# Loads of q and k issued two chunks ahead, and the first strided stores, the mask and half of the first values put on GpSimd's queue

## The chip, the cores and the metric

The kernel runs on one core of one Trainium2 chip. The metric is the device time in microseconds (us) of one execution, lower is better. The kernel before takes 826.1 us in the median of three runs (820.74 to 828.68). The core has five instruction streams that run side by side: PE (TensorE: matrix multiplies and transposes), ACT (ScalarE), DVE (VectorE), POOL (GpSimd) and SP (SyncE, which only issues transfers here). Each stream is in order: an instruction that waits holds everything behind it on its own engine.

## The reference

Attention with two kinds of windows feeds a mixture of experts with one expert per token, and that feeds a last layer with a rational activation. Cut to what matters:

```
scores = q k^T / 8, for 4 batches, 8 heads, 576 positions, 64 elements a head
heads 0-3: each position sees the last 32 positions
heads 4-7: each position sees every fourth of the last 128
attn = softmax(scores) ; x = attn v, rows of 512 elements, 2304 tokens
logits = x w_gate + modality_bias ; e = argmax(logits)
x = gate * relu(x w1[e]) w2[e]          # 8 experts, 512 -> 1024 -> 512
h = x w_in ; g = P(h) / (Q(h) + 1e-6) ; out = g w_out
```

## The kernel before

**Chunks.** The attention runs over 8 chunks. A chunk is two batches and two heads; its kind (table `CHUNKS`, line 34) is 1 for the strided heads and 0 for the plain ones. Chunks 0 and 1 are strided, 2 and 3 plain, 4 and 5 strided, 6 and 7 plain. Chunks 0 to 3 belong to batches 0 and 1 (`bp` 0), the others to batches 2 and 3 (`bp` 1). `load(c)` (line 408) brings q and k of a chunk into a pair of tiles from the pool `ald`, which has two buffers (line 388), so a chunk's tiles can be filled when the chunk two before it has been read for the last time. A strided chunk comes as rows of 2 KB (72 partitions), a plain one as pieces of 256 bytes. `load_values(c)` (line 427) brings v into one of two buffers `vws`; for strided heads one call brings all four heads (`load_v_dil`, 12 transfers), for plain heads two at a time (`load_v`, 2 transfers). `halo(c)` (line 449) then copies, on POOL, the last 32 rows of each block to the top of the next one.

**The loop.** 36 steps g (line 635) each work on 4 tiles of 64 positions. A step issues up to two parts of `qk_T` (PE transposes of the loaded q or k, ACT copies them out), `step_s` for tile group g (scores on PE, mask and maximum on DVE, line 489), `step_e` for g-1 (exponentials on ACT), `step_t` for g-2 (transposes on PE), `step_v` for g-3 (product with v on PE, line 515, and scaling on DVE into the tile `xu`, line 529). When four heads of a batch pair are done, `put_x` (line 585) stores `xu` to the DRAM tensor `x_rows`: for strided heads as 20 transfers on SP, because neighbouring positions of a head lie four rows apart in `x_rows`; `xu` has two buffers. `gate_tasks` puts the router's work between the steps. At the end of a step, the loop decides which loads to issue: `load(done_L)` once 8(done_L-1) parts of `qk_T` have been issued (line 679), values once the steps have come far enough (line 682).

**Order.** The block is scheduled by hand: each engine runs its instructions in the order in which the code issues them. Transfers issued by SP and ACT share eight completion semaphores (DMAHW0 to DMAHW7 in the rows of order below). A transfer that is given a semaphore first waits until the transfer that held it before has landed; usually that is the one eight before it. Transfers issued by POOL have eight of their own (DMASW).

**Start.** `load(0)` issues q on SP and k on ACT, in halves (one head, both batches), with the mask on ACT between them; then come the 12 transfers of the first values and `load(1)` on SP. `spin` runs empty multiplies on PE between the first parts of `qk_T` (`SPIN`, line 84).

**End of the attention.** After the last step ACT issues the two halves of the first expert's second weight, `raw20` and `raw21` (1 MB each, `fetch2`, line 213), and then runs the last `step_e` (line 696). The rest of the kernel, from about 160 us on, is the experts and the last layer; their first weights and gathers are released by the router's result.

Of the kernel before, what the change touches and what calls it, by code (L numbers as in the profile page):

```python
# [18 lines left out]
B, H, S, D = 4, 8, 576, 64  # L19
NTOK = B * S  # L20
DM = H * D
QT, WIN, KT = 64, 32, 96
NJ = S // QT
# [7 lines left out]
CQ = 16  # L31
RUNS = ((0, 2), (2, 3), (3, 4), (4, 5), (5, 6), (6, 7), (7, 9))
# [51 lines left out]
SPIN = (12, 0, 1, 0)  # L84
# [82 lines left out]
def fused(ctx, tc, io):  # L167
# [215 lines left out]
    with ExitStack() as actx, tc.manual_schedule(), nc.allow_low_precision(reason="integers"):  # L383
# [24 lines left out]
        def load(c):  # L408
            bp, _, kind, h0 = CHUNKS[c]
            raw[c] = [ld.tile([72, 2, 2, 8 * D] if kind else [QT, 2 * NJ, 2, D], F32, tag="ld" + nm, name="ld" + nm) for nm in "qk"]  # L410
            bs = slice(2 * bp, 2 * bp + 2)
            if c == 0:
                for hh in range(2):
                    for t, src, eng in zip(raw[c], (q, k), (nc.sync, nc.scalar)):
                        eng.dma_start(out=t[:, hh], in_=src[bs, h0 + hh].rearrange("b (p j) d -> p b (j d)", j=8))
                    if hh == 0:
                        nc.scalar.dma_start(out=mask[:, 0:NP0], in_=io["mask"][:, 0:NP0])
                return
            for t, src in zip(raw[c], (q, k)):
                for bb in range(2):  # L420
                    x = src[2 * bp + bb, h0:h0 + 2]
                    if kind:
                        nc.sync.dma_start(out=t[:, :, bb, :], in_=x.rearrange("h (p j) d -> p h (j d)", j=8))
                    else:
                        nc.sync.dma_start(out=t[:, :, bb, :], in_=x.rearrange("h (j a) d -> a (h j) d", a=QT))
# [8 lines left out]
        def load_v_dil(bp, vw):  # L434
            for j in range(NJ):
                for lo, hi in pieces(QT * j, QT * j + QT):
# [5 lines left out]
                    nc.sync.dma_start(out=vw[a:a + hi - lo, :, j, 1:1 + 2 * D], in_=src)  # L442
# [142 lines left out]
        def put_x(c):  # L585
            bp, _, kind, _ = CHUNKS[2 * c]
            xu = xus.pop(c)
            cols = slice(DM // 2 * kind, DM // 2 * kind + DM // 2)
            for hf in range(2):
                xb = xu[64 * hf:64 * hf + 64].rearrange("a j h d -> a j (h d)")  # L590
                if not kind:
                    b = 2 * bp + hf
                    nc.sync.dma_start(out=x_dram[b * S:(b + 1) * S, cols].rearrange("(j a) e -> a j e", a=QT), in_=xb)
                    continue
                rr = x_dram[2 * bp * S:(2 * bp + 2) * S, cols].rearrange("(b m r) e -> b r m e", b=2, r=4)
                for j0, j1 in RUNS:
                    for lo, hi in ([(QT * j0, QT * j1)] if j1 - j0 == 2 else pieces(QT * j0, QT * j1)):
                        sg, m = divmod(lo, SEG)
                        bb, r2 = divmod(sg, 2)
                        dst = rr[bb, 2 * r2 + hf, m:m + hi - lo]  # L600
                        if j1 - j0 == 2:
                            nc.sync.dma_start(out=dst.rearrange("(j a) e -> a j e", a=QT), in_=xb[:, j0:j1])
                        else:
                            a = 64 * hf + lo - QT * j0
                            nc.sync.dma_start(out=dst, in_=xu[a:a + hi - lo, j0].rearrange("a h d -> a (h d)"))
# [10 lines left out]
        halo(0)  # L616
        load(1)
        load_values(1)
        halo(1)
# [15 lines left out]
        for g in range(NG):  # L635
# [43 lines left out]
            if done_L < NC and done_T >= 8 * (done_L - 1):  # L679
                load(done_L)  # L680
                done_L += 1
# [950 lines left out]
```

## Time and profile before

| | |
|---|---|
| median of 3 runs | 826.1 us (820.74 to 828.68) |
| the profiled execution | 826.8 us, of which the span from the first to the last instruction is 825.0 us |
| mean granted TensorE clock | 0.979 of full |
| PE busy | 791.3 us (96%) |
| PE weight loads busy | 638.4 us (77%) |
| DVE, ACT, POOL busy | 577.6, 509.7, 149.0 us |
| transfers | 73509 packets, 91.58 MB |

"Busy" adds up the time in which an engine had an instruction at work; times in the rows count from the span's start. The chain of waits is followed back from the last instruction of the kernel, so what stands in it held up the end. The attention takes about the first 140 us of the span; the change touches nothing behind it.

### The profile page before, as it was taken

The page shows a single profiled execution, that of the slowest core. Times are in us where ns is not written, and L with a number is a line of the kernel's source. Part 1 is how long each engine was busy: PE and PEld are TensorE (multiplying, and loading weights), DVE is VectorE, ACT ScalarE, POOL GpSimd, SP SyncE. Part 2 cuts the span into 40 slices and gives each one's busy share as a digit, 9 for nine tenths or more (in the row PEclk, how much of TensorE's full clock was granted, in tenths as well). Part 3 has the DMA queues.
Part 4 walks back from the last instruction along what each step waited for, and adds up shares of the span by engine and source line. Part 5 has one row for each costly group of instructions (what it writes and reads, how often), then busy time and mean ns, then how long its engine had stood idle before and what let it go on. Part 6 is the DMA issues. An engine that isn't in the chain of part 4 may idle for free.

```text
span 825.0 us, 15207 instructions
## 1 busy us (share of the span) xinstructions
PE 791.3 (96%) x5277; PEld 638.4 (77%) x5279; DVE 577.6 (70%) x1370; ACT 509.7 (62%) x993; POOL 149.0 (18%) x191
## 2 busy tenths in 40 slices
PE   7899997899998999999989999999999999999995
PEld 4777765687786678888768888888888888999894
DVE  3776788932252224895599987887788888888894
ACT  4655666234253325663689878777687678778783
POOL 2011008421110101231174512000020002001001
PEclk9998899999999999999999999999999999999998
DMA  7968947195947686774011001200020001001001
GB/s 189 160 145 150 191 147 199 51 339 211 333 153 288 247 306 209 236 276 158 18 39 39 14 1 38 66 1 1 0 69 22 1 0 65 1 1 38 1 1 38
DMA packets 73509, 91.58 MB, mean 111 GB/s; under 512 B 33577, under 2 KB 43323, under 8 KB 73403
## 3 DMA queue, kind: packets, MB, share of 16 engines
q1 hardware_dynamic: 68531, 76.38, 32.7%
q0 software_dynamic: 3360, 11.03, 3.8%
q10 hardware_dynamic: 1512, 2.91, 1.1%
q8 instruction: 48, 0.79, 0.4%
q14 instruction: 58, 0.48, 0.2%
HBM read 75.59 MB, written 14.71 MB: 109 GB/s over the span
## 4 chain that ended last, share of the span: by engine, by line
PE 83%; DMA 8%; DVE 4%; ACT 3%; issue 1%; SPq 0%; POOL 0%; POOLq 0%; ACTq 0%; DVEq 0%
PE p1t L1363 8%; PE p1t L1364 8%; PE p1t L1365 8%; DMA sw<-in_w 5%; PE p1t L146 4%; PE p1t L150 4%; PE p1t L148 4%; PE pht L1533 4%; PE pht L1534 3%; PE pht L1535 3%; PE pot L777 3%; PE pot L775 3%; PE pot L779 3%; PE pot L1535 2%; PE pxt L1533 2%; PE pxt L1534 2%
## 5 line engine op out<-in xcount | busy, mean ns | idle before, releaser
L1481 ACT ACTIVATE raw<-p1t 128x512 f32<-128x512 f32 (+1 forms) x78 | 43.2, 554 | 81.9 <-PE p1t L1365 77.0
L1488 DVE TENSOR_TENSOR raw<-raw,raw 128x512 f32<-128x512 f32 (+1 forms) x80 | 52.0, 649 | 59.0 <-ACT raw L1482 58.2
L768 DVE TENSOR_TENSOR hl<-pht,hh 128x512 fp32r<-128x512 f32 x34 | 21.9, 685 | 97.9 <-ACT hh L767 92.7
L1365 PE MATMUL p1t<-yh,wl 128*128 128x512 f32 (+1 forms) x240 | 89.0, 371 | 0.0
L1544 POOL DMA_INDIRECT out<-hs,row x10 | 10.9, 1087 | 302.2 <-ACT hs L1542 300.8
L1482 ACT ACTIVATE raw<-raw,bab 128x512 f32<-128x512 f32 (+1 forms) x80 | 61.9, 773 | 2.7
L1363 PE MATMUL p1t<-yh,wh 128*128 128x512 f32 (+1 forms) x160 | 59.6, 372 | 0.3 <-DVE m L1499 0.3
L1364 PE MATMUL p1t<-yl,wh 128*128 128x512 f32 (+1 forms) x160 | 59.2, 370 | 0.0
L1510 DVE SCALAR_TENSOR_TENSOR m<-m,nab,raw 128x512 f32<-128x512 f32 (+1 forms) x80 | 58.6, 733 | 0.1
L146 PE MATMUL p1t<-w1h,xh 128*128 128x512 f32 x144 | 57.7, 401 | 0.1
L150 PE MATMUL p1t<-w1h,xl 128*128 128x512 f32 x144 | 56.7, 393 | 0.0
L148 PE MATMUL p1t<-w1l,xh 128*128 128x512 f32 x144 | 56.4, 392 | 0.0
L1508 DVE SCALAR_TENSOR_TENSOR raw<-raw,raw 128x512 f32<-128x512 f32 (+1 forms) x80 | 56.4, 705 | 0.0
L1483 ACT ACTIVATE raw<-p1t,nab 128x512 f32<-128x512 f32 (+1 forms) x78 | 56.1, 719 | 0.0
L1490 ACT ACTIVATE raw<-raw,bab 128x512 f32<-128x512 f32 (+1 forms) x80 | 53.7, 671 | 0.5 <-DVE raw L1488 0.4
L1499 DVE SCALAR_TENSOR_TENSOR m<-m,nab,p1t 128x512 f32<-128x512 f32 (+1 forms) x78 | 53.5, 685 | 0.1
L775 PE MATMUL pot<-w2h,hh 128*128 128x512 f32 x128 | 52.0, 406 | 0.0
L777 PE MATMUL pot<-w2l,hh 128*128 128x512 f32 x128 | 51.6, 403 | 0.0
L1506 DVE SCALAR_TENSOR_TENSOR raw<-raw,raw 128x512 f32<-128x512 f32 (+1 forms) x80 | 51.6, 645 | 0.0
L1497 DVE TENSOR_TENSOR m<-raw,p1t 128x512 f32<-128x512 f32 (+1 forms) x78 | 49.3, 632 | 2.7
L779 PE MATMUL pot<-w2h,hl 128*128 128x512 f32 x128 | 50.6, 395 | 0.0
L489 DVE CUSTOM_DVE_ANT_0 pe<-sc,mask 128x96 f32<-128x96 f32 x144 | 28.4, 253 | 31.6 <-PE sc L485 19.6
(374 smaller groups left out, 2110.5 us busy)
## 6 DMA issues: line engine op xcount, KB each, us to landing
sw<-in_w SPq DMA_DIRECT2D x80, 256.0 KB
raw<-in_w SPq DMA_DIRECT2D x10, 1024.0 KB
dr<-in_w_in SPq DMA_DIRECT2D x16, 512.0 KB
dr<-in_w_out SPq DMA_DIRECT2D x16, 512.0 KB
y<-ys_rows SPq DMA_DIRECT2D x18, 256.5 KB
ldq<-in_q SPq DMA_DIRECT2D x16, 288.0 KB
ys_rows<-yo SPq DMA_DIRECT2D x17, 256.5 KB
ldk<-in_k SPq DMA_DIRECT2D x14, 288.0 KB
```

The source lines that it names most:

```text
L146: nc.tensor.matmul(out=p, lhsT=xh[:, kk], rhs=wh[n][:, kk], start=(kk == 0), stop=False)
L148: nc.tensor.matmul(out=p, lhsT=xh[:, kk], rhs=wl[n][:, kk], start=False, stop=False)
L150: nc.tensor.matmul(out=p, lhsT=xl[:, kk], rhs=wh[n][:, kk], start=False, stop=(kk == 3))
L775: nc.tensor.matmul(out=p, lhsT=a[:, c], rhs=w2h[n][:, kk], start=(c == 0), stop=False)
L777: nc.tensor.matmul(out=p, lhsT=a[:, c], rhs=w2l[n][:, kk], start=False, stop=False)
L779: nc.tensor.matmul(out=p, lhsT=b[:, c], rhs=w2h[n][:, kk], start=False, stop=(c == 7))
L1363: nc.tensor.matmul(out=p[:, 0:n], lhsT=wh(kk)[:, cs], rhs=ab[0][:, kk, 0:n], start=(kk == 0), stop=False)
L1364: nc.tensor.matmul(out=p[:, 0:n], lhsT=wh(kk)[:, cs], rhs=ab[1][:, kk, 0:n], start=False, stop=False)
L1365: nc.tensor.matmul(out=p[:, 0:n], lhsT=wl(kk)[:, cs], rhs=ab[0][:, kk, 0:n], start=False, stop=(kk == 3))
L1482: nc.scalar.activation(out=v, in_=ah, func=AF.Identity, scale=bab[:, 1:2], bias=bab[:, 0:1])
L1508: nc.vector.scalar_tensor_tensor(out=v, in0=v, scalar=2.0, in1=r, op0=ALU.subtract, op1=ALU.mult)
L1510: nc.vector.scalar_tensor_tensor(out=m, in0=m, scalar=nab[:, 0:1], in1=v, op0=ALU.add, op1=ALU.mult)
```

## The change

The diff, with lines of the loop that are only indented anew left out. `load(0)` issues quarters (one head, one batch) and the mask goes first, on POOL. Of the first values, odd blocks j go through POOL's queue. The strided `put_x` stores both halves (the two heads' parity rows) of a block with one transfer where the block lies within one segment, so 18 transfers instead of 20, and for batches 0 and 1 on POOL's queue. `halo(0)` is issued behind `load(1)`. `load(done_L)` is issued one chunk earlier in the code. The number of buffers in the pool `ald` isn't in the diff: it is two in both kernels.

```diff
-SPIN = (12, 0, 1, 0)
+SPIN = (12, 2, 2, 2)
...
             if c == 0:
+                nc.gpsimd.dma_start(out=mask[:, 0:NP0], in_=io["mask"][:, 0:NP0])
                 for hh in range(2):
-                    for t, src, eng in zip(raw[c], (q, k), (nc.sync, nc.scalar)):
-                        eng.dma_start(out=t[:, hh], in_=src[bs, h0 + hh].rearrange("b (p j) d -> p b (j d)", j=8))
-                    if hh == 0:
-                        nc.scalar.dma_start(out=mask[:, 0:NP0], in_=io["mask"][:, 0:NP0])
+                    for bb in range(2):
+                        for t, src, eng in zip(raw[c], (q, k), (nc.sync, nc.scalar)):
+                            eng.dma_start(out=t[:, hh, bb], in_=src[2 * bp + bb, h0 + hh].rearrange("(p j) d -> p (j d)", j=8))
                 return
...
         def load_v_dil(bp, vw):
             for j in range(NJ):
+                eng = nc.gpsimd if bp == 0 and j % 2 else nc.sync
...
-                    nc.sync.dma_start(out=vw[a:a + hi - lo, :, j, 1:1 + 2 * D], in_=src)
+                    eng.dma_start(out=vw[a:a + hi - lo, :, j, 1:1 + 2 * D], in_=src)
...
-                for j0, j1 in RUNS:
-                    for lo, hi in ([(QT * j0, QT * j1)] if j1 - j0 == 2 else pieces(QT * j0, QT * j1)):
...
+            eng = nc.sync if bp else nc.gpsimd
+            rr = x_dram[2 * bp * S:(2 * bp + 2) * S, cols].rearrange("(b m r) e -> b r m e", b=2, r=4)
+            for j in range(NJ):
+                parts = pieces(QT * j, QT * j + QT)
+                for lo, hi in parts:
+                    sg, m = divmod(lo, SEG)
+                    bb, r2 = divmod(sg, 2)
+                    dst = rr[bb, 2 * r2:2 * r2 + 2, m:m + hi - lo]
+                    if len(parts) == 1:
+                        eng.dma_start(out=dst, in_=xu[:, j].rearrange("a h d -> a (h d)"))
+                        continue
+                    for hf in range(2):
+                        a = 64 * hf + lo - QT * j
+                        eng.dma_start(out=dst[hf], in_=xu[a:a + hi - lo, j].rearrange("a h d -> a (h d)"))
...
-        halo(0)
         load(1)
         load_values(1)
+        halo(0)
         halo(1)
...
-            if done_L < NC and done_T >= 8 * (done_L - 1):
+            if done_L < NC and done_T >= 8 * (done_L - 2):
                 load(done_L)
```

SP's queue before, from the load of chunk 2 on (`ldq`, `ldk` are the tiles of q and k, `vw1` and `vw0` the two buffers of values; 64x18x64 is a plain chunk, 72x2x512 a strided one):

```order
L425 DMA ldq_302<-in_q 64x18x64 x2
L425 DMA ldk_303<-in_k 64x18x64 x2
L446 DMA vw1_153<-in_v 64x18x64 x2
L425 DMA ldq_551<-in_q 64x18x64 x2
L425 DMA ldk_552<-in_k 64x18x64 x2
L446 DMA vw1_153<-in_v 64x18x64 x2
L423 DMA ldq_816<-in_q 72x2x512 x2
L423 DMA ldk_817<-in_k 72x2x512 x2
L602 DMA x_rows_57<-xu_392 64x2x256
L605 DMA x_rows_57<-xu_392 16x256
```

Behind these come the other stores of `xu` (20 in all), the 12 transfers of the next values, and only then chunk 5. The same place on SP's queue in the change:

```order
L422 DMA ldq_277<-in_q 64x18x64 x2
L422 DMA ldk_278<-in_k 64x18x64 x2
L422 DMA ldq_317<-in_q 64x18x64 x2
L422 DMA ldk_318<-in_k 64x18x64 x2
L444 DMA vw1_153<-in_v 64x18x64 x4
L420 DMA ldq_570<-in_q 72x2x512 x2
L420 DMA ldk_571<-in_k 72x2x512 x2
L420 DMA ldq_831<-in_q 72x2x512 x2
L420 DMA ldk_832<-in_k 72x2x512 x2
L440 DMA vw0_152<-in_v 64x4x128 x2
```

Chunks 2 and 3 now stand ahead of both loads of plain values, chunks 4 and 5 ahead of the next strided values, and the stores of `xu` are gone from this queue. They stand on POOL's queue in the change, between small copies and the halo copies of the next strided values (`vw0`):

```order
L260 CAST tok16_97<-cst_82 128x9
L602 DMA x_rows_57<-xu_407 2x64x256 x2
L606 DMA x_rows_57<-xu_407 16x256 x2
L606 DMA x_rows_57<-xu_407 48x256 x2
L602 DMA x_rows_57<-xu_407 2x64x256
L606 DMA x_rows_57<-xu_407 32x256 x4
L602 DMA x_rows_57<-xu_407 2x64x256
L606 DMA x_rows_57<-xu_407 48x256 x2
L606 DMA x_rows_57<-xu_407 16x256 x2
L602 DMA x_rows_57<-xu_407 2x64x256 x2
L451 COPY vw0_152<-vw0_152 32x8x128 x4
```

Before, the four halo copies of `vw0` followed the small copies directly. On ACT, at the end of the loop, the two halves of the first expert's second weight and the last exponentials, before:

```order
L213 DMA raw20_2278<-in_w2 128x4x512
L213 ISA
L213 DMA raw21_2279<-in_w2 128x4x512 [waits DMAHW5_49]
L496 ACTIVATE pe_2346<-pe_2346,mx_2347 128x96 [waits DVE_49] x4
L130 ACTIVATE w1h1_2272<-raw11_66 128x512 [waits DMAHW4_49,DMAHW3_49,DMAHW0_49]
```

And in the change:

```order
L211 DMA raw20_2283<-in_w2 128x4x512 [waits DMAHW5_49]
L211 ISA
L211 DMA raw21_2284<-in_w2 128x4x512 [waits DMAHW5_49]
L494 ACTIVATE pe_2351<-pe_2351,mx_2352 128x96 [waits DVE_49] x4
L128 ACTIVATE w1h1_2277<-raw11_66 128x512 [waits DMAHW7_49,DMAHW6_49,DMAHW3_49]
```

Before, the two halves held different semaphores (`raw20` DMAHW7, `raw21` DMAHW5). In the change both hold DMAHW5, so `raw21` waits until `raw20` has landed, and the exponentials stand behind it.

## Rows read from the trace of the kernel before

**Rows 1.** The page's chain that ended last, by engine.
```profile
PE 83%; DMA 8%; DVE 4%; ACT 3%; issue 1%; SPq 0%; POOL 0%; POOLq 0%; ACTq 0%; DVEq 0%
```

**Rows 2.** Stretches: bounds, length, busy us (count) by engine, PE clock, DMA share, GB/s.
```profile
59.60:69.10 9.50, 9.50 (x175) 8.30 (x176) 8.29 (x52) 7.80 (x27) 0.00 (x0) 1.00 0.42 115
76.20:89.90 13.70, 13.16 (x130) 9.70 (x126) 5.80 (x31) 5.52 (x18) 0.00 (x0) 0.50 1.13 172
126.00:136.00 10.00, 7.26 (x89) 5.36 (x89) 8.60 (x35) 7.14 (x18) 9.32 (x10) 0.83 0.82 269
```

**Rows 3.** The chain's pieces in the attention: start us, us, what.
```profile
1.86 8.95 DMA ldk<-in_k
14.92 5.59 DMA ldk<-in_k
22.63 6.59 DMA ldq<-in_q
69.72 5.65 DMA ldq<-in_q
131.41 1.02 PE pt L503 x4
```

**Rows 4.** SP's transfers in order of time: start us, us, line, count.
```profile
13.87 1.01 SPq L423 DMA_DIRECT2D ldq<-in_q  x2
21.91 1.45 SPq L425 DMA_DIRECT2D ldq<-in_q  x2
...
44.67 0.63 SPq L602 DMA_DIRECT2D x_rows<-xu  x1
...
59.63 6.77 SPq L442 DMA_DIRECT2D vw<-in_v  x9
...
69.14 0.96 SPq L423 DMA_DIRECT2D ldq<-in_q  x2
```

**Rows 5.** DVE's first mask operation of steps 16, 20, 24 and 25.
```profile
60.25 0.26 DVE L489 CUSTOM_DVE_ANT_0 pe<-sc,mask 128x96 f32<-128x96 f32 x1
70.94 0.26 DVE L489 CUSTOM_DVE_ANT_0 pe<-sc,mask 128x96 f32<-128x96 f32 x1 [0.39 <-PE sc L485]
90.31 0.26 DVE L489 CUSTOM_DVE_ANT_0 pe<-sc,mask 128x96 f32<-128x96 f32 x1 [2.10 <-ACT pe L496]
94.03 0.25 DVE L489 CUSTOM_DVE_ANT_0 pe<-sc,mask 128x96 f32<-128x96 f32 x1
```

**Rows 6.** PE: the product of step 12, the router's multiply, two waits for q.
```profile
47.67 0.69 PE L515 MATMUL pv<-vw,pts 96*64 96x65 f32 x16
69.42 0.85 PE L562 MATMUL lgp<-xT,wg 128*32 128x384 f32 x6
73.65 0.47 PE L463 MATMUL pq<-ident,ldq 72*128 72x72 f32 x4 [1.22 <-DMA ldq<-in_q]
```

**Rows 7.** POOL: halo copies, the last small copy, its only transfers before 130 us.
```profile
36.07 2.02 POOL L453 COPY vw<-vw 32x1024 f32<-32x1024 f32 x2 [16.99 <-DMA vw<-in_v]
47.92 2.02 POOL L453 COPY vw<-vw 32x1024 f32<-32x1024 f32 x2 [9.83 <-DMA vw<-in_v]
...
51.52 0.20 POOL L262 CAST tok<-cst 128x9 f16<-128x9 f32 x1
...
123.88 1.14 POOL L365 DMA_INDIRECT xg<-x_rows,idx  x1 [16.14 <-DVE mx L489]
125.32 0.96 POOL L365 DMA_INDIRECT xg<-x_rows,idx  x1 [0.31 <-PE pg L549]
```

**Rows 8.** ACT and SP at the end of the attention.
```profile
126.97 0.42 ACTq L213 DMA_DIRECT2D raw<-in_w  x1
129.37 1.17 ACT L496 ACTIVATE pe<-pe,mx 128x96 f32<-128x96 f32 x4 [0.46 <-DVE mx L489]
...
133.34 4.22 SPq L605 DMA_DIRECT2D x_rows<-xu  x7
```

**Rows 9.** SP's own waits, 100 to 140 us: us in total, times, longest.
```profile
SPq L605 <- DMA raw<-in_w: 20.4, 2, 16.5
```

More of the change, by code (lines that the diff above doesn't have):

```diff
@@ L28 @@
 HP = HT + 1
-CQ = 16
-RUNS = ((0, 2), (2, 3), (3, 4), (4, 5), (5, 6), (6, 7), (7, 9))
 KINDS = ((1, 1, 0, 0), (1, 1, 0, 0))
@@ L410, in load @@
             raw[c] = [ld.tile([72, 2, 2, 8 * D] if kind else [QT, 2 * NJ, 2, D], F32, tag="ld" + nm, name="ld" + nm) for nm in "qk"]
-            bs = slice(2 * bp, 2 * bp + 2)
             if c == 0:
+                nc.gpsimd.dma_start(out=mask[:, 0:NP0], in_=io["mask"][:, 0:NP0])
                 for hh in range(2):
-                    for t, src, eng in zip(raw[c], (q, k), (nc.sync, nc.scalar)):
-                        eng.dma_start(out=t[:, hh], in_=src[bs, h0 + hh].rearrange("b (p j) d -> p b (j d)", j=8))
-                    if hh == 0:
-                        nc.scalar.dma_start(out=mask[:, 0:NP0], in_=io["mask"][:, 0:NP0])
+                    for bb in range(2):
+                        for t, src, eng in zip(raw[c], (q, k), (nc.sync, nc.scalar)):
+                            eng.dma_start(out=t[:, hh, bb], in_=src[2 * bp + bb, h0 + hh].rearrange("(p j) d -> p (j d)", j=8))
                 return
@@ L588, in put_x @@
             cols = slice(DM // 2 * kind, DM // 2 * kind + DM // 2)
-            for hf in range(2):
-                xb = xu[64 * hf:64 * hf + 64].rearrange("a j h d -> a j (h d)")
-                if not kind:
+            if not kind:
+                for hf in range(2):
                     b = 2 * bp + hf
-                    nc.sync.dma_start(out=x_dram[b * S:(b + 1) * S, cols].rearrange("(j a) e -> a j e", a=QT), in_=xb)
-                    continue
-                rr = x_dram[2 * bp * S:(2 * bp + 2) * S, cols].rearrange("(b m r) e -> b r m e", b=2, r=4)
-                for j0, j1 in RUNS:
-                    for lo, hi in ([(QT * j0, QT * j1)] if j1 - j0 == 2 else pieces(QT * j0, QT * j1)):
[L598 to L605, printed above, removed]
+                    nc.sync.dma_start(out=x_dram[b * S:(b + 1) * S, cols].rearrange("(j a) e -> a j e", a=QT),
+                                      in_=xu[64 * hf:64 * hf + 64].rearrange("a j h d -> a j (h d)"))
+                return
+            eng = nc.sync if bp else nc.gpsimd
[9 more added lines that the diff above has]
+                        continue
+                    for hf in range(2):
+                        a = 64 * hf + lo - QT * j
+                        eng.dma_start(out=dst[hf], in_=xu[a:a + hi - lo, j].rearrange("a h d -> a (h d)"))
         for i in range(NB):
```

## The prediction

> **What bounds the kernel now.** I read the chain of waits first. Over the whole span it runs on PE for 83% and through transfers for 8% [rows 1]; the question is where in the attention those transfers hold PE up, because the change touches nothing behind it. The pieces of the chain show four such places [rows 3]. The second half of the first k is issued at 1.86 and lands at 10.81. The k of chunk 1 is issued at 14.92 and lands at 20.51. The q of chunk 2 (22.63) lands at 29.22. The q of chunk 5 (69.72) lands at 75.37. The first three are one string. SP can't issue chunk 1 before 13.87 [rows 4], because five loads of the first values still stand ahead of it when the first k lands: (13.87 - 10.82) / 5 = 0.61 us each. Chunk 2's q, at 21.91 [rows 4], waits for chunk 1's last k, whose completion semaphore it takes.
>
> The fourth place is the costly one. Chunk 5 is issued only at 69.14, behind the stores that began at 44.67 and the values that began at 59.63 [rows 4]. PE then waits 1.22 us for it [rows 6], and from 76.2 to 89.9 its granted clock is 0.50, that is 1.2 GHz, with PE busy for 13.16 of 13.70 us [rows 2]. Just before, from 59.6 to 69.1, PE had been busy all the time at full clock while the 16 transfer engines were used for 0.42 [rows 2]. So there the transfers are late because of the order on SP's queue and the waits in it, not because the engines are full.
>
> What that costs is read off DVE's first mask operation, one per step. From step 16 to step 20 a step takes (70.94 - 60.25) / 4 = 2.67 us. From step 20 to step 25 the five take 94.03 - 70.94 = 23.09 us [rows 5]. Undisturbed I expect four at 2.67, one router multiply of 0.85 [rows 6], and the last at the 94.03 - 90.31 = 3.72 us that it already takes at full clock: 15.25. The place costs 7.8 us. Its lower bound, half of the slowed PE time alone, is 13.16 / 2 = 6.6.
>
> **The change part by part.** All sums are against the profiled execution, 826.8 us with a span of 825.0; the median of the runs shown, 826.1, is 0.7 lower.
>
> *Start: quarters, mask on POOL, half of the values on POOL, more spins.* Quarters let PE begin before 6.9 us, but that gain isn't kept: PE still waits for chunk 2's q in step 7, and what counts is when SP issues chunk 1. Eight of the twelve loads of values remain on SP, and only the last of them still needs a semaphore that the late q and k hold. So four fewer stand behind the landing: 4 x 0.61 = 2.4 us. The last quarter of q may land a little ahead of the last half of k, up to 0.9 more. Against it, POOL's four loads now share the transfer engines with q and k; that is at worst their own share of the time, 1 us. Bounds 1.4 to 3.3; I take **2.6**. The five extra spins fill time in which PE would wait. The same 2.6 carries through the string to step 8, since its members wait for each other.
>
> *Loads two chunks ahead.* The code issues them earlier, but the pool still has two buffers. A load therefore waits on SP for the last transposes of the chunk two before, as now, and what moves is only the order. What this frees: chunk 5 now waits for chunk 3's last transposes, about 58 - 2.6 = 55 us, instead of 69.14. It has about 15 us to land, where the four transfers of chunk 1 took 8 us beside other work. The wait at 73.65 and the slow clock behind it should go: **7.8**.
> What it delays: the first plain values, now behind chunk 3. Chunk 2's q, k and values needed 36.07 - 21.91 = 14.2 us and chunk 3's 47.92 - 36.07 = 11.9 [rows 4, 7]. Two thirds of the latter, 7.9, now go first, so these values land at 36.07 - 2.6 + 7.9 = 41.4, and one halo copy of 1.0 us later step 12 can use them. It wants them at 47.67 - 2.6 = 45.1 [rows 6]. Cost nothing, with 2.7 us to spare. The stores of chunks 2 and 3 and the plain values of chunk 6 stand behind chunk 7's load, which can go when chunk 5 is read out, near 80. By the same rates the load takes 7.9 and the values 4.0, and I allow 3 for the stores: 95. Step 30 wants these values five steps of about 3 us behind step 25 (94.03 - 10.4 = 83.6), near 98.6. Again no cost.
>
> *Stores on POOL.* SP loses 20 stores that took it from 44.67 to 59.6. POOL gets 18, behind its halo copies and small copies. Those end at 51.72 now [rows 7], so at 49.1. The next halo copies, which step 21 needs, stand behind the stores, and so does the release of the buffer of `xu`. Step 21's mask would run at 70.94 + 2.67 - 2.6 = 71.0 and its product with the new values 0.6 later, at 71.6 (an estimate: four transposes lie between). With a time r per store, the copy must fit: 49.1 + 18 r + 1.0 <= 71.6, r <= 1.19. No row shows a direct store issued by POOL. The nearest are two indirect transfers of 128 rows: 0.96 and 1.14 us, 1.44 from start to start [rows 7]. Twelve of the 18 stores have 16 to 48 rows, so I take r = 1.0 and **no cost**, with 3 us of room. At 1.44 the copy is 4.5 us late; then PE idles again and part of the 7.8 goes with it.
>
> A page of the Trainium skill speaks against this part. "DMA: Bandwidth & Descriptors", section "Issuing engines are not separate DMA queues", holds that issuing from several engines saves only the sequencer's time, usually small beside the transfer. The transfer engines at 0.42 while chunk 5 stands in SP's queue say that here it isn't small [rows 2, 4]. By that rule alone, the place at 70 us would stay as it is.
>
> *End of the attention.* Here the order shows a new wait. `raw21` now takes the semaphore that `raw20` holds, so ACT stands still until `raw20` has landed, and the last exponentials wait behind it. Now `raw20` is issued at 126.97 and the exponentials run at 129.37 [rows 8]. With both halves in flight `raw20` lands at 133.3, where a store on SP that waited for it goes on [rows 8, 9]: 6.4 us, the upper bound. Alone, 1.05 MB at the 269 GB/s of this stretch [rows 2] take 3.9, the lower. I take 5.0: ACT is free at 132.0, with its second issue (0.42) at 132.4, 3.0 later than now. PE's transposes at 131.41 [rows 3] follow the end of the exponentials (130.54) with 0.9 to spare, so 2.1 us are lost, and some at the low clock that PE already has there (0.83 on average [rows 2]). I take **2.5**, bounds 1 to 5. `raw21` itself isn't needed sooner.
>
> *Later strided stores (batches 2, 3).* 18 transfers instead of 20 on SP, far ahead of their use. Nothing.
>
> **Sum.** 2.6 + 7.8 - 2.5 = 7.9 us gained: 826.8 - 7.9 = **818.9 us**. Behind the attention everything is released by the router's result, so I let the gain through whole.
>
> **The rivals.**
> - *POOL is a little slow (r from 1.2 to 1.5).* Its stores take the place of the removed wait in step 21: up to 4.8 us of idle PE, and the clock may fall as it did behind 1.2 us of waiting. For it: indirect transfers 1.44 apart. Against it: twelve short stores. 818.9 + 4 = 823, or with the slow clock (6.6 us) up to 829.
> - *POOL is slow (r near 2): slower than before.* One mechanism: 18 stores end at 85.1 and the halo copy at 86.1, 14.5 us behind step 21's need. 818.9 + 14.5 + 4 of slow clock = 837. It decides from r = 1.6, where the copy is late by the 7.9 us of the gain. Against it: no transfer on POOL in these rows takes 2 us.
> - *Transfers are hidden or bound anyway; the change does not do what it says.* The two buffers forbid a real lead of two chunks. If the engines, busy for 1.13 of their time (summed over transfers) from 76 to 90 us [rows 2], are the limit, chunk 5 stays late and only start and end change: 826.8 - 2.6 + 2.5 = 826.7. Against it the 0.42.
> - *The start gains more and the end costs little:* 3.3 + 8.5 - 1 = 10.8, that is 816; with PE's clock kept up in the first 15 us a little less still.
>
> **How the numbers follow.** Chances: the forecast 0.50 (its own range 816.5 to 821.5), start and end better 0.18 (813 to 816.5), POOL a little slow 0.16 (822 to 829), transfers bound 0.08 (about 826.7), POOL slow 0.08 (832 and up). The range 813 to 829 leaves out POOL slow and the tails of the others. Measured against 826.1, 1% (about what a measurement of this kernel can tell) ends at 817.8 and 834.4. Faster by more holds the better case and two fifths of the forecast, 0.18 + 0.2, rounded to 0.40; slower by more 0.08 to 0.10; the rest is within 1%, 0.50.
>
> **What would show it.** Right, in the profile after: chunk 1 issued near 11.3; chunk 5 issued near 55 and no wait of PE for q near 70; PE's clock full from 15 to about 120; 18 direct transfers on POOL, about 1 us each, ending before 69; an idle ACT of about 3 us before the last exponentials. Wrong: halo copies of `vw0` ending after 72, PE waiting for v in step 12 or 21, the clock at 0.50 anywhere between 15 and 115, or an attention that is shorter by 8 us with a kernel that isn't, which would mean that the experts' part takes the gain back.

## The result, and the profile after

The changed kernel is slower than the one before: the ratio of the times is **1.0077, with a 95% interval from 1.0048 to 1.0105**, from 12 runs of each (runs over 1.5% above the fastest of the same kernel are left out of every ratio here). The medians of all runs are 830.16 us after (826.86 to 835.67) and 827.62 us before (820.18 to 833.53). The prediction was 818.9 us, with a range from 813 to 829, so the median lies 11.3 us above the forecast and 1.2 above the range, on the other side of no change.

| | before | after |
|---|---|---|
| profiled execution | 826.8 us | 835.7 us (the longest of its 12 runs) |
| its span | 825.0 us | 833.8 us |
| mean granted PE clock | 0.979 | 0.969 |
| PE busy | 791.3 us | 795.1 us |
| POOL busy | 149.0 us | 163.4 us |

The chain of waits by engine covers less than half of the span in this trace, so, unlike [rows 1], it can't be used to rank the waits:

```profile
PE 46%; ACT 2%; DVE 1%; POOL 0%; issue 0%; POOLq 0%; ACTq 0%
```

I go by the six views that answer to [rows 2] and [rows 4 to 8] instead. First the three stretches of [rows 2] (bounds, length, busy us with counts of PE, PEld, DVE, ACT, POOL, PE clock, DMA share, GB/s), now of after:

```profile
59.60:69.10 9.50, 9.50 (x180) 8.28 (x179) 8.46 (x50) 6.89 (x23) 5.42 (x9) 1.00 0.90 217
76.20:89.90 13.70, 11.06 (x112) 8.70 (x112) 5.51 (x31) 4.72 (x14) 3.98 (x4) 0.62 0.46 80
126.00:136.00 10.00, 5.89 (x79) 4.36 (x78) 7.97 (x38) 3.08 (x8) 7.58 (x8) 0.73 0.45 144
```

From 59.6 to 69.1 the transfer engines are used for 0.90 where they were for 0.42 [rows 2]. From 76.2 to 89.9 the clock is not full: 0.62, after 0.50. From 126 to 136 ACT is busy for 3.08 us where it was for 7.14. SP's transfers of after in order of time (start us, us to issue, line, count):

```profile
13.72 1.01 SPq L420 DMA_DIRECT2D ldq<-in_q  x2
...
55.50 1.00 SPq L420 DMA_DIRECT2D ldq<-in_q  x2
...
59.89 1.11 SPq L420 DMA_DIRECT2D ldk<-in_k  x2
61.10 12.18 SPq L440 DMA_DIRECT2D vw<-in_v  x12
73.40 2.47 SPq L422 DMA_DIRECT2D ldq<-in_q  x2
```

Chunk 1 is issued at 13.72, where [rows 4] had 13.87. Chunk 5's q is issued at 55.50 and no longer at 69.14, its k 4.4 us later. The values of chunk 4 stand behind that k and are issued from 61.10 to 73.3; before, the twelve began at 59.63 and took 9.42 (the row in [rows 4] ends after nine of them):

```profile
59.63 9.42 SPq L442 DMA_DIRECT2D vw<-in_v  x12
```

DVE's first mask operations of steps 16, 20, 24 and 25, as in [rows 5]:

```profile
61.55 0.26 DVE L487 CUSTOM_DVE_ANT_0 pe<-sc,mask 128x96 f32<-128x96 f32 x1
72.23 0.26 DVE L487 CUSTOM_DVE_ANT_0 pe<-sc,mask 128x96 f32<-128x96 f32 x1 [0.39 <-PE sc L483]
92.43 0.26 DVE L487 CUSTOM_DVE_ANT_0 pe<-sc,mask 128x96 f32<-128x96 f32 x1 [2.23 <-ACT pe L494]
96.55 0.25 DVE L487 CUSTOM_DVE_ANT_0 pe<-sc,mask 128x96 f32<-128x96 f32 x1
```

Steps 20 to 25 take 24.3 us (23.1 before). Of PE: the transposes of chunk 5's q, the product of step 21 with the new values, and the last transposes of the attention:

```profile
73.56 0.41 PE L461 MATMUL pq<-ident,ldq 72*128 72x72 f32 x4
...
78.84 0.57 PE L513 MATMUL pv<-vw,pts 96*64 96x65 f32 x12 [3.29 <-POOL vw L451]
...
139.73 1.25 PE L501 MATMUL pt<-ident,pe 128*96 128x128 f32 x4 [5.61 <-ACT pe L494]
```

The wait for q at 73.65 [rows 6] is gone, and a wait of 3.29 us for values stands 5 us behind its place. POOL's first strided stores, two of their issues, and the halo copies that PE waits for:

```profile
54.32 2.06 POOL L606 DMA_DIRECT2D x_rows<-xu  x4
...
67.14 1.77 POOL L602 DMA_DIRECT2D x_rows<-xu  x2
...
77.76 3.98 POOL L451 COPY vw<-vw 32x1024 f32<-32x1024 f32 x4 [8.85 <-DMA vw<-in_v]
```

POOL was done with issuing the stores at 68.9. It then waited 8.85 us for the values and copied them from 77.76 on. Before, the same copies stood at 70.76:

```profile
70.76 3.96 POOL L453 COPY vw<-vw 32x1024 f32<-32x1024 f32 x4 [19.04 <-DMA vw<-in_v]
```

And ACT at the end of the attention, the counterpart of [rows 8]:

```profile
130.96 1.14 ACT L128 ACTIVATE w1h<-raw 128x512 fp32r<-128x512 f32 x2
132.34 6.92 ACTq L211 DMA_DIRECT2D raw<-in_w  x2
139.30 1.17 ACT L494 ACTIVATE pe<-pe,mx 128x96 f32<-128x96 f32 x4 [7.21 <-DMA raw<-in_w]
```

ACT stands still for 7.21 us with the last exponentials behind `raw21`, and PE's transposes for 5.61 behind these.

Where after lies behind before, by the same rows: 1.3 us at step 20 (72.23 against 70.94), 2.5 at step 25 and 2.5 at step 35, then 8.3 at the last transposes (139.73 against 131.41 [rows 3]), 6.9 at the last transfer to the output, and 8.8 at the end of the span (8.9 in the whole time).

### The profile page after: what moved, and what is told of

The parts are those of the page before. It is cut to its first block, busy times and chain, and to the rows that moved or that the text cites. A ratio compares the mean times of both kernels' runs of the same rounds, so it can differ in the third digit from the quotient of the medians.

```text
span 833.8 us, 15249 instructions
## 1 busy us (share of the span) xinstructions
PE 795.1 (95%) x5284; PEld 642.0 (77%) x5284; DVE 577.2 (69%) x1370; ACT 509.9 (61%) x993; POOL 163.4 (20%) x214
## 5 line engine op out<-in xcount | busy, mean ns | idle before, releaser
L1364 PE MATMUL p1t<-yh,wh 128*128 128x512 f32 (+1 forms) x160 | 59.6, 372 | 0.3 <-DVE m L1500 0.3
L1366 PEld LDWEIGHTS p1t<-yh,wl 128*128 128x128 f32 x240 | 45.0, 188 | 6.9 <-POOL wl L1417 0.7
```

The lines of the kernel that those rows point to most:

```text
L1364: nc.tensor.matmul(out=p[:, 0:n], lhsT=wh(kk)[:, cs], rhs=ab[0][:, kk, 0:n], start=(kk == 0), stop=False)
L1366: nc.tensor.matmul(out=p[:, 0:n], lhsT=wl(kk)[:, cs], rhs=ab[0][:, kk, 0:n], start=False, stop=(kk == 3))
```

## The experiments

Theories after the result. **E**: the shared semaphore at the end costs most of the loss, about 6 us, since `raw20` is now issued right ahead of the exponentials and not 2.4 us earlier. **O**: the values of chunk 4 land late because SP's queue holds them behind a load that waits for one of two buffers. Rivals: **P**, POOL's stores fill the transfer engines and make the values late whatever SP's order is, and **C**, PE's clock falls near 76 whatever the kernel does there.

**`raw21` issued behind the last exponentials.**

```diff
-        for n in range(2):
-            fetch2(n, e, nc.scalar)
+        fetch2(0, e, nc.scalar)
         step_e(NG - 1)
         split1(2)
+        fetch2(1, e, nc.scalar)
```

> The changed kernel with one edit: ACT issues raw21 behind the last exponentials and the two weight conversions that follow them, instead of ahead of them. In the trace of after, ACT stood still for 7.21 us with the last exponentials (139.30) until raw20 had landed, and PE's transposes of these came at 139.73 against 131.34 before; the lag of after behind before grew there from 2.5 to 8.9 us. Theory A (that stall is on the path in every execution and nothing gives it back): 6 us less than after, that is about the time of before (827.6), ratio to before 1.000, and no idle ACT ahead of the last exponentials. Theory A' (the size in my prediction): 2.5 us less than after, ratio 1.005. Rival (the experts' part hides it, because its first products wait for the weights that raw20 and raw21 bring in any case): as after, ratio 1.008.

Measured: 0.9994 [0.9960, 1.0028] to before, 0.8% less than after. ACT's rows:

```profile
129.55 0.43 ACTq L211 DMA_DIRECT2D raw<-in_w  x1
131.26 0.41 ACTq L211 DMA_DIRECT2D raw<-in_w  x1
131.33 0.90 ACT L494 ACTIVATE pe<-pe,mx 128x96 f32<-128x96 f32 x3
```

No wait for `raw20` is left, and with it the whole loss against before is gone, though the order at 70 to 90 is still that of after. E holds.

**The values ahead of chunk 5's load, by the old condition.**

```diff
-            if done_L < NC and done_T >= 8 * (done_L - 2):
+            if done_L < NC and done_T >= 8 * (done_L - 1):
```

> The changed kernel with the old condition for the loads of q and k (one chunk ahead), so that SP issues the strided values of chunk 4 ahead of chunk 5's q and k. In the trace of after these values are issued from 61.10 to 73.29, behind a k load that waits until 59.89 for its buffer; they land at 78.09, POOL's halo copies end at 81.7 and PE stands 3.29 us before the products of step 21; from 76 to 90 the clock is 0.62. Theory B (order on SP's queue, a wait for a buffer ahead of values that need none): values issued near 47 to 58, landed by 62, no wait for the halo copies, clock 1.0 from 76 to 90, steps 20 to 25 in about 16 us instead of 24.3; 8 us less than after, ratio about 0.998. Rival B' (the transfer engines, at 0.90 from 59.6 to 69.1, are the limit, with POOL's stores beside the loads): something else is late by the same amount (chunk 5 or the values), as after, ratio 1.008. Rival B'' (SP then brings chunk 5 as late as in the kernel before): a wait for q near 70 and the clock at 0.50 again, ratio about 1.005.

Measured: 1.0033 [0.9995, 1.0072]. The stretch, POOL's halo copies and the exponentials:

```profile
76.20:89.90 13.70, 12.20 (x196) 9.41 (x194) 10.83 (x64) 8.28 (x27) 1.45 (x2) 1.00 1.06 196
...
68.16 3.98 POOL L451 COPY vw<-vw 32x1024 f32<-32x1024 f32 x4
...
128.50 1.17 ACT L494 ACTIVATE pe<-pe,mx 128x96 f32<-128x96 f32 x4 [6.79 <-DMA raw<-in_w]
```

With POOL's stores unchanged the copies run at 68.16 without a wait, and the clock is full from 76 to 90. Step 35 begins at 121.31 where it began at 129.09 before. So C is wrong, and so is P in the form that the values are late whatever SP's order is; what the shared engines add is taken up below. But the end still has its wait of 6.79, and the time came out above what was expected.

**Three buffers for q and k.** `bufs=3` for the pool `ald`, nothing else.

> The changed kernel with three buffers in the pool of q and k instead of two, so that a load two chunks ahead really finds a free buffer. SP's order stays that of after. Theory B: the k load of chunk 5 no longer stops SP until 59.89, the values behind it go at about 50 to 58 and land by 65, and the place near 76 us disappears as in the run with the old condition; 8 us less than after, ratio 0.998, chunk 5 issued near 47. Rival B' (transfer engines are the limit): all loads move forward into the stretch with POOL's stores, each takes longer, and the values come as late; as after, 1.008.

Measured: 1.0036 [0.9998, 1.0074]. Chunk 5 is issued at 44.88 and holds nothing up, and ACT's wait at the end is 7.69. The same place is mended in another way, with the same time. Both runs are some 3.5 us below after (1.0077), with intervals that overlap.

**The start as before, the rest as after** (halves, the mask on ACT, all values on SP, the old `SPIN`, the old place of `halo(0)`).

> The changed kernel with the first loads as before: q and k of chunk 0 in halves, mask on ACT's queue, all first values on SP, the old number of idle products, the halo copies in their old place. My prediction's step for the start (2.6 us gained by the edits): 2.6 us more than after, ratio 1.011. Rival C (the trace of after: chunk 1 is issued at 13.72 as before at 13.87, and steps 0 to 20 run 1.1 to 1.3 us later than before): 1.3 us less than after, ratio 1.006, step 0 near 11.1, step 20 near 70.9. Rival D (the place at 76 us absorbs a lag of the start, since its values wait on SP): as after, 1.008.

Measured: 1.0122 [1.0077, 1.0168], 3.7 us more than after, with intervals that overlap. Its trace has the wait of ACT too (7.26). The size of the start is taken up below.

**The late stores back to 20 transfers.**

```diff
         def put_x(c):
             bp, _, kind, _ = CHUNKS[2 * c]
+            if kind and bp == 1:
+                put_old(c)
+                xus.pop(c)
+                return
```

> The changed kernel with only the late strided stores (batches 2 and 3, on SP) as before: 20 transfers in place of 18, same bytes. My prediction gave this edit nothing. Completion semaphores are handed out in turn, eight of them; with 18 transfers raw20 and raw21 get the same one, with 20 they get two. Theory A (the stall of ACT at the end comes from that count alone): no wait of ACT for raw20, 6 us less than after, ratio to before 1.000, as with raw21 issued behind the exponentials. Rival: the smaller stores cost SP as much again and the result stays as after, 1.008.

(`put_old`, not shown, issues the 20 transfers of before on SP.) Measured: 0.9987 [0.9946, 1.0027]. ACT's rows:

```profile
125.84 0.43 ACTq L213 DMA_DIRECT2D raw<-in_w  x1
126.45 0.41 ACTq L213 DMA_DIRECT2D raw<-in_w  x1
127.35 1.16 ACT L496 ACTIVATE pe<-pe,mx 128x96 f32<-128x96 f32 x4
```

Two more transfers in SP's queue give `raw20` and `raw21` different semaphores again (numbers 115 and 113 in the records of this trace, 115 twice in after), and the wait is gone. The gain is that of the first experiment.

**Only the late stores changed.** Before, with the 18 transfers for batches 2 and 3 on SP.

> The kernel before with one part of the change alone: the late strided stores (batches 2 and 3) in 18 transfers on SP. It too gives raw20 and raw21 one completion semaphore. Theory A: the last exponentials wait for raw20 (idle ACT of about 7 us ahead of them, about 139 us), ratio 1.008 (6 us slower than before). My prediction's size: 2.5 us, ratio 1.003. Rival: nothing, 1.000.

Measured: 1.0056 [1.0021, 1.0092].

```profile
126.40 0.42 ACTq L213 DMA_DIRECT2D raw<-in_w  x1
134.68 0.39 ACTq L213 DMA_DIRECT2D raw<-in_w  x1
135.12 1.17 ACT L496 ACTIVATE pe<-pe,mx 128x96 f32<-128x96 f32 x4 [7.80 <-DMA raw<-in_w]
```

This one edit alone makes the kernel slower by 4.6 us. All five traces with the 18 transfers and `raw21` in its old place (after, the second to fourth experiment, this one) show 6.79 to 7.80 us of idle ACT there, and in each the records of the two issues name one semaphore. None of the other traces has the wait, and in none that holds both records do they name the same one. In the trace, SP's stores go round the eight semaphores in a fixed turn and leave out the places of `raw20` and `raw21`: seven stores lie between these two places in after and here, so that the turn comes back to the same semaphore, and five in before and in the run above. What puts the two places so far apart isn't shown.

**Both mended** (the old condition and the 20 late transfers), run twice.

> The changed kernel with the old load condition (as in the second run) and the late stores in 20 transfers (as in the run beside this). In the trace with the old load condition alone, step 35 stood at 121.31 against 129.09 before, 7.8 us ahead, and PE's transposes of the last exponentials only 2.4 us ahead, since ACT waited 6.8 us for raw20. Theory A+B (two separate losses of after: order on SP's queue at 76 us, shared semaphore at the end): with both gone the 7.8 us arrive behind the attention and at the end: ratio 0.991 (820). Rival E (the experts' part takes an earlier start back, because it waits for its weights' transfers): ratio 0.996 to 1.000 though the attention ends 7 us earlier. Rival (the gain at 76 us is mostly lost again by other waits before the end): the attention itself ends less than 4 us earlier.

> The same kernel as the run with the old load condition and 20 late stores (0.9981, runs from 815.6 to 831.4, profiled execution 820.2 with the clock never low between 1 and 122 us), to see a second execution and twice the runs. Theory L: if this profiled execution is a slow one (825 or more), its clock is at 0.50 for tens of us somewhere in the attention before 76 us; if it is a fast one, it is not. Rival E (the experts' part takes the gain back): a slow execution whose attention ends as early as 122 to 125 us. Ratio again 0.995 to 1.000.

Measured: 0.9981 [0.9930, 1.0031], then 0.9965 [0.9937, 0.9993]. The expectation of about 0.991 was missed: in the first one's trace steps 20 to 25 take 7.3 us less than in [rows 5], and the runs show a gain of 1.6 and 2.9 us. Beside the run with the 20 late transfers alone (0.9987), the mended order adds 0.5 us in the first.

**Only POOL's stores for batches 0 and 1 changed**, from before.

> The kernel before with one part of the change alone: the strided stores of batches 0 and 1 in 18 transfers on POOL's queue; loads one chunk ahead, first loads and late stores as before. It differs from the run with the old condition and 20 late stores by the start's edits alone. Theory B: SP is free of stores from 44 to 60, the values of chunk 4 land by 62 and chunk 5 by 70, the wait for q at 73.65 and the slow clock from 76 to 90 are gone: 7.8 us less than before, ratio 0.991, if the end lets it through. For the start, between this and its neighbour: my prediction says the neighbour is 2.6 us faster; rival C (the start's edits cost 1.3 us, as the steps of after show) says this one is 1.3 us faster; the run with the old start in the changed kernel (1.0122 against 1.0077) says 3.7 us for the neighbour.

Measured: 1.0004 [0.9962, 1.0047]. Steps 20 and 25:

```profile
71.82 0.26 DVE L489 CUSTOM_DVE_ANT_0 pe<-sc,mask 128x96 f32<-128x96 f32 x1 [0.39 <-PE sc L485]
...
87.69 0.25 DVE L489 CUSTOM_DVE_ANT_0 pe<-sc,mask 128x96 f32<-128x96 f32 x1
```

The span of this execution is 819.0, the clock is full from 56 to 115, steps 20 to 25 take 15.9 us, and yet the runs show nothing. So the 7.8 us of the prediction were not there to be had in the runs. The next runs ask why.

**The kernel before, traced twice more.**

> The kernel before once more, for its profile alone. Theory L says that the slow clock from 76 to 90 us on which my 7.8 us rested belongs to one execution: here the clock may be low elsewhere (20 to 55) or nowhere in the attention, and the steps 20 to 25, 23.1 us there, take 17 to 19 without it (the wait of 1.2 us for q stays). Rival: each execution of this kernel has the slow clock at 76 to 90 and the 23 us.

> The kernel before a third time, for its profile alone; the same question as in the run beside it: whether the clock is at 0.50 from 76 to 90 us in each execution (rival) or at places that differ from one execution to the next (theory L).

The first took 827.43 us. Two stretches, and the first mask operations of steps 20 and 25:

```profile
30.00:44.00 14.00, 14.00 (x146) 10.96 (x142) 7.77 (x45) 6.21 (x20) 2.02 (x2) 0.50 1.26 163
76.20:89.90 13.70, 13.40 (x240) 10.87 (x238) 11.30 (x67) 9.97 (x34) 3.97 (x4) 1.00 0.95 153
...
83.36 0.26 DVE L489 CUSTOM_DVE_ANT_0 pe<-sc,mask 128x96 f32<-128x96 f32 x1 [0.39 <-PE sc L485]
...
99.35 0.25 DVE L489 CUSTOM_DVE_ANT_0 pe<-sc,mask 128x96 f32<-128x96 f32 x1
```

The second took 817.23 us:

```profile
30.00:44.00 14.00, 12.89 (x197) 9.41 (x197) 10.04 (x59) 9.91 (x32) 2.02 (x2) 1.00 1.30 168
76.20:89.90 13.70, 11.46 (x170) 8.33 (x171) 8.36 (x46) 7.66 (x25) 0.00 (x0) 1.00 1.12 174
...
71.69 0.26 DVE L489 CUSTOM_DVE_ANT_0 pe<-sc,mask 128x96 f32<-128x96 f32 x1 [0.39 <-PE sc L485]
...
90.06 0.25 DVE L489 CUSTOM_DVE_ANT_0 pe<-sc,mask 128x96 f32<-128x96 f32 x1
```

One program, three courses. Steps 20 to 25 take 23.1 us in the first trace [rows 5], 16.0 here in the one whose clock had been at 0.50 already from 22 to 56, and 18.4 in the one that had no fall between 16 and 118. PE is so late in the second that the transfers are in time. In the third it still waits 0.92 us for chunk 5, and the clock stays full.

**The clock held up at the start.** Both mended, with two idle products of 288 columns ahead of each group of early transposes of three heads.

> The changed kernel with the old load condition and 20 late stores, and besides with two idle products of 288 columns on PE ahead of each group of transposes of the second unit, of the third unit (chunk 1) and of the q and k of chunk 2, where PE waits 0.5 to 1.1 us for transfers in the steps 0 to 8. They compute nothing that is used. In the traces so far the granted clock fell to 0.50 early in some executions for 34 us (20.7 to 54.8 and 21.8 to 55.9 in two runs, 34.2 to 51.3 in a third), and not in others with nearly the same waits; the runs of one kernel spread over 16 us along with their mean clock. Theory L (the medians hide the gain at 76 us because such an early fall, which the wait at 76 us used to absorb, now costs its full time): with PE busier ahead of it the fall becomes rarer, the slow runs above 825 us thin out and the ratio comes to 0.991 to 0.994. Rival (the falls don't depend on these gaps): the same spread as without the filling, 0.998, or slower by the filling itself (up to 3 us).

Measured: 0.9993 [0.9963, 1.0023], against 0.9965 without the fillers, measured beside it. The mean clock was 0.985 or more in ten of twelve runs, but the shortest runs were some 2 us longer than without them. Inconclusive: it doesn't show that the early fall can be kept off at a profit.

**Only the mask on POOL**, from before, one execution.

> The kernel before with one transfer moved: the first part of the mask is issued on POOL's queue, not on ACT's. In all traces so far the span goes on for 8.30 us behind PE's last product where POOL issues only indirect transfers (three executions of the kernel before, and the late stores alone), and for 10.15 to 10.25 us where POOL also issues direct ones (after and eight other runs, with 18 to 23 of them); the last output lands 2.7 us behind its issue in both. Theory P (a fixed price at the end for having used direct transfers on POOL at all): 10.2 us behind the last product with this one transfer. Rival (the price comes with their number): near 8.4. Rival (it comes from something else in those kernels, such as the order of the semaphores): 8.30.

Measured: 825.97 us. It has the fall from 75 to 89, a wait of 3.0 us for chunk 5's q, and 23.8 us for steps 20 to 25, like before. It was meant for the end of the kernel, below.

**The order alone, with nothing on POOL.** Before, with the first strided stores still on SP as 20 transfers, but behind chunk 4's values and chunk 5's load, and three buffers of `xu`.

```diff
-                    put_x(c)
+                    if c == 0:
+                        late.append(c)
+                    else:
+                        put_x(c)
...
                 load(done_L)
+                if done_L == 6:
+                    put_x(late.pop())
```

> The kernel before with one edit: the strided stores of batches 0 and 1 stay on SP, but stand behind the values of chunk 4 and behind chunk 5's load there (with a third buffer for xu, so that they may go later). Nothing is issued on POOL but the indirect transfers. Theory B (order on SP's queue is what holds chunk 5): values issued from about 44, chunk 5 near 60, no wait for q near 74, steps 20 to 25 in 15.5 to 16.5 us where they take 18.4 in the undisturbed execution of the kernel before, and 8.30 us behind the last product: 2 to 3 us less than before, ratio 0.9965 or less, and no loss at the end. Rival F (the stores now hold chunk 6, which stands behind them): chunk 6 issued near 76 instead of 71, a wait for its q near step 24 or 25, ratio 1.000 to 1.004.

Measured: 0.9953 [0.9914, 0.9991]. The traced execution is a long one, 830.37 us, with the clock at 0.50 from 22 to 56. SP's rows:

```profile
54.13 7.39 SPq L442 DMA_DIRECT2D vw<-in_v  x12
...
66.71 0.75 SPq L423 DMA_DIRECT2D ldq<-in_q  x2
...
71.95 0.62 SPq L605 DMA_DIRECT2D x_rows<-xu  x1
```

What this place gives needs the order (and here a third buffer of `xu`, not tried by itself) and no second queue: POOL's stores alone gave 1.0004 above, of whose distance 1.9 us is the end of the program (last section). The Trainium skill's "DMA: Bandwidth & Descriptors", section "Issuing engines are not separate DMA queues", says that transfers of all issuing engines run on the same 16 transfer engines, and that issuing from several saves only the sequencer's time. This run agrees with the second, and the DMA share of 0.90 in after with the first.

**The change with both faults taken out**: three buffers and the 20 late transfers.

> The changed kernel with three real buffers for q and k and with the late stores in 20 transfers, so that raw20 and raw21 have two semaphores. The run with three buffers alone gave 1.0036, with ACT waiting 7.69 us for raw20. Theory A (6 us for the shared semaphore, whatever stands ahead): ratio 0.996 to 0.997, as with the old condition and 20 stores (0.9981 and 0.9965), no wait of ACT for raw20. Rival (the earlier loads take the gain back in the steps 0 to 15): 1.000.

Measured: **0.9939 [0.9903, 0.9975]**, median 820.47 against 824.38. SP's rows and DVE's of steps 20 and 25:

```profile
42.79 1.23 SPq L422 DMA_DIRECT2D ldq<-in_q  x2
...
46.26 16.28 SPq L442 DMA_DIRECT2D vw<-in_v  x12
...
69.47 0.26 DVE L489 CUSTOM_DVE_ANT_0 pe<-sc,mask 128x96 f32<-128x96 f32 x1 [0.39 <-PE sc L485]
...
85.30 0.25 DVE L489 CUSTOM_DVE_ANT_0 pe<-sc,mask 128x96 f32<-128x96 f32 x1
```

The values go out from 46.26 on, with no load at the head of the queue that waits for a buffer. Steps 20 to 25 take 15.8 us, and ACT doesn't wait for `raw20` at the end. This is the fastest version, by 0.6% against before; its interval overlaps that of the run above.

## Why the prediction was wrong

The forecast for the profiled execution was 16.8 us short (835.7 - 818.9). By its own steps: 3.9 at the start (1.3 late at step 20, where 2.6 early was said), 9.0 at the place near 70 to 90 (1.2 lost where 7.8 were to be gained), and 3.9 from step 25 to the end (6.4 lost instead of 2.5). The steps that failed: the late stores, put at "Nothing", cost 4.6 us by themselves; the list of what the earlier loads delay left out chunk 4's values, for which PE waits 3.29 us; and the 7.8 us were read from one execution and taken as the kernel's.

**The end: the mechanism was right, the size was not.** The prediction saw that `raw21` would wait for `raw20` and that the exponentials stand behind it, and charged 2.5 us. The runs put it at 4.6 to 7.4: 0.8 and 0.9% for taking it out of after in two ways, 0.56% for putting it into before, 5.9 us of lag between step 35 and the last transposes in the trace. Two terms were wrong. The sum let `raw20` start at 126.97, ahead of the last steps' exponentials; in after it starts at 132.34, right behind the conversion at 130.96, and no lead is left. And it took 5.0 us for the transfer to land; in after it took 6.5 (ACT's row for both issues, 6.92 less the second issue of 0.41), close to the 6.4 us read from SP's row, which the prediction had kept as the upper bound; with the late stores alone it took 8.3 (126.40 to 134.68). The cause lies in an edit that the prediction dismissed with "Nothing": the late stores, 18 transfers instead of 20. The number of stores moved the turn of the semaphores, so a count on SP decides what ACT waits for. The prediction tied the wait to the change as a whole and never to this line.

**The place at 70 to 90: the step "what moves is only the order" failed.** It is right that chunk 5 is issued at 55 (55.50) and that PE doesn't wait for it. The prediction followed POOL's queue to the halo copies and found 3 us of room. On SP's it listed the plain values of chunks 2 and 6 as delayed and left out those of chunk 4. Chunk 5's k takes its buffer at 59.89, when the last transposes of chunk 3's k are done, and the values of chunk 4, which do not need that buffer, stand behind it. They share the engines with POOL's stores and land near 78, where the forecast had the halo copies done by 71.6. The hold on SP's queue is the smaller part against before: the values start 1.5 us later than there (61.10 against 59.63), their last issue ends 4.2 later, and the copies start 7.0 later (77.76 against 70.76); the rest lies behind the issue, with the transfer engines used for 0.90 where it was 0.42. What the right order does is to let the values go ahead of that crowd: from 44.35 in the second experiment's trace. That the prediction looked for lateness in the time r per store sent it to the wrong queue: r was 0.5 to 0.9 us, better than the 1.0 taken, and it didn't matter. The rival "POOL a little slow" gave the right symptom, halo copies late and a slow clock behind the wait, by the wrong cause.

**And the 7.8 us were one execution's.** With the order mended, steps 20 to 25 take 15.5 to 16.8 us in eight traces, near the predicted 15.25. With the order of after they took 24.3 and 22.2, and 15.5 twice, with `raw21` moved and with the old start, where the clock had been at its lower level from 22 to 54 or longer. In the five traces with the order of before at this place the same steps took 23.1 and 23.8 us (before, and with only the mask on POOL), 18.4 (the one without a fall), and 16.0 and 15.8 (before again and with only the late stores changed, both with the clock at its lower level for 17 us or more ahead of 56). The clock's fall is not bound to a wait of 1.22 us, as the prediction took it to be: in the second experiment PE waits as long, and the clock is full from 76 to 90.

```profile
77.99 0.69 PE L513 MATMUL pv<-vw,pts 96*64 96x65 f32 x16 [1.22 <-DVE xu L527]
```

Undisturbed, the place costs about 3 us (18.4 - 15.3); the rest comes and goes with the clock, and in before an early fall hides the wait at 76, which it can't do where the wait is gone. So versions without the wait at the end that begin step 35 from 6.2 to 10.4 us earlier than before's first trace gain 0 to 5 us in the runs. Of what is missing, 1.9 us is the end of the program (last section).

The clock's share can be read from the runs, each of which has its mean clock on record. Among runs at 0.984 or more, the medians are 819.2 to 820.2 us in the four sets of before (8, 6, 4 and 1 runs), 817.4, 818.6 and 819.0 in the three of versions with both faults taken out (each 0.5 to 2.1 less than before beside it), and 814.5 where SP's order alone was changed (three runs). So at a high clock the mended change gains little net of its longer end. But 21 of its 37 runs have that clock, and 19 of 110 of before: most of the rest of its gain lies in how often the clock stays up. Why it does isn't shown; no run holds the clock still.

**The start.** Chunk 1 was to be issued at 11.3 and came at 13.72. The term of five loads at 0.61 us counts issue time only; and not one but four of SP's eight value loads wait for semaphores that quarters of q and k hold, the last for a quarter of q that lands near 13.1. POOL's mask and four value loads share the engines with it, which the prediction had priced at 1 us at worst. In traces without the early fall and with two buffers, step 8 begins at 34.1 to 34.3 in three with the new start (33.7 with the fillers) and at 35.6 in after, and at 34.6 to 35.5 in three with the old: about 1 us of 2.6. In the runs it is 3.7 us (the fourth experiment) and 1.9 (both mended, against POOL's early stores alone), each within its intervals. Between 0 and 3.7 stays open.

**What held.** PE didn't wait for the plain values, though their copies began at 44.06 where the forecast had them landed at 41.4; 18 stores on POOL were issued by 68.9; the clock is full from 56 to 115 wherever the order is mended. "The gain passes through whole" is open: of 8.3 us of lag at the last transposes 6.9 are left at the last output transfer, but clocks differ on the way.

## What to carry to other kernels

Follow every queue that a reordering touches, not only the one that gains work: a load that is issued early but waits for a buffer holds all that stands behind it on its engine. Where transfers are given their completion semaphores in turn, a changed count of transfers elsewhere can change who waits for whom; look at the two or three large transfers issued just ahead of critical work on an in-order engine, and give them the price of a whole landing. Before a gain is read from a stretch at half clock, trace the same kernel again: a fall of the clock seen in one execution need not be a property of the code ahead of it.

## What was not expected of the hardware

**The end of the program grows with POOL's direct transfers.** The last transfer to the output, of before, of the kernel with only the mask on POOL, of the one with only the early stores there, and of after:

```profile
819.65 0.99 POOL L1544 DMA_INDIRECT out<-xg,row  x1 [0.28 <-POOL row L1543]
```

```profile
818.75 0.98 POOL L1544 DMA_INDIRECT out<-xg,row  x1 [0.28 <-POOL row L1543]
```

```profile
811.71 0.99 POOL L1573 DMA_INDIRECT out<-xg,row  x1 [0.28 <-POOL row L1572]
```

```profile
826.59 0.98 POOL L1545 DMA_INDIRECT out<-xg,row  x1 [0.28 <-POOL row L1544]
```

To the end of their spans (825.0, 824.2, 819.0, 833.8) it is 5.35, 5.45, 7.29 and 7.21 us. With 18 or more direct transfers on POOL the kernel ends 1.9 us later behind the same last transfer; with one it is 0.1. All traces of versions with 18 to 23 such transfers show it, and none without them. Whether their number or their packets set it wasn't tried. The prediction charged POOL's stores with nothing.

**PE's clock can stay at its lower level for long, early, with PE busy.** In 6 of 17 traces the granted clock is 0.50, which is 1.2 GHz, for 17 to 34 us between 20 and 56 us, as from 30 to 44 us in the second trace of before above, where PE is busy for 14.00 of 14.00 us. The third trace of the same program has 1.00 there with PE busy for 12.89. In the second trace of the version with both faults mended:

```profile
30.00:44.00 14.00, 13.80 (x142) 10.47 (x143) 6.77 (x41) 6.71 (x21) 2.02 (x2) 0.55 1.26 169
```

What decides it is open. The runs of each kernel spread over 5 to 18 us (one run of before, 846.90 us, apart), the longer ones at the lower mean clock: beside the last version, before took 817.83 us at 0.983 and 829.59 at 0.964.
